# One routed tile's weight loads, a small tile's fetch and a routing table at other places in an attention and experts kernel

## The chip, the cores and the metric

The program runs on one core of a Trainium2 chip. The metric is the time of one execution in microseconds of the device, the median of several runs. One execution was also taken by the hardware profiler; all times inside the program are from that one, in microseconds from the start of its span.

TensorE is called PE in the views (PEld for its weight loads), VectorE DVE, ScalarE ACT, GpSimd POOL and SyncE SP. SP computes nothing here; it issues DMAs, in the order of the program.

## What is computed

Three stages, in float32: attention with rotated queries and keys (2 batches, 8 heads, 576 positions, 64 wide), a dense layer pair with softplus between, and a routed layer: every one of the 1,152 tokens with a positive score goes to one of 8 experts, and its expert's result is added to it.

```python
def _moe2_ref(x, w_skip, w_gate, w1, w2):
    do_compute = x @ w_skip > 0
    out = x.copy()
    xc = x[do_compute]
    logits = xc @ w_gate
    e_idx = np.argmax(logits, axis=1)
    probs = softmax(logits)
    gate_w = probs[np.arange(len(xc)), e_idx]
    for e in range(E):
        mask = e_idx == e
        h = np.maximum(xc[mask] @ w1[e], 0.0)      # w1[e]: 512 x 1024
        y[mask] = gate_w[mask, None] * (h @ w2[e]) # w2[e]: 1024 x 512
    out[do_compute] = xc + y
    return out
```

(`softmax` stands for the four lines that compute it.)

## The kernel before

Attention and the dense pair fill the first 380 us and are not touched. The rows that the dense pair gives are written to a table in DRAM, `x2d` (each with its gate and its number behind it), 128 rows at a time, and to `out`.

**Routed tiles.** Tokens are sorted by expert into tiles of 128 rows. A tile has one expert. What is left of an expert over full tiles and is at most 32 rows goes into small tiles, four parts of an expert's width by 32 rows. The program has seven full tiles in its straight path (tile 0 and tiles 1 to 6) and two small ones; further ones stand behind a branch. Which expert a tile has is known only when the routing is done: SP reads two values of `ei` for a tile, the expert and whether it differs from the tile before (`values`, L1184).

**Weights.** An expert's weights are eight chunks of 512 KB, in eight buffers `raw[0]` to `raw[7]`: 0 to 3 are of w1, 4 to 7 of w2. `load_chunk` (L947) issues one DMA on SP's queue. `load(T, chunks)` (L973) does so under the condition that tile T has another expert than T - 1; otherwise the DMA moves nothing, but it still is issued in its turn and waits for its buffer. Four further buffers, `sraw`, are for the small tiles.

A product in full precision is made of three with shorter operands. So a chunk is split: ScalarE copies its high half (`split_w`, L959), VectorE subtracts that from the chunk for the low half (`low_w`, L967). Chunk 0 of tiles 1 and later is used as it lies (`AS_IS`), in a slower product. A tile's rows are fetched from `x2d` by an indirect DMA of GpSimd (`fetch`, L979; `small_fetch` for a small tile), turned by PE (`rows`, `xgt` in the views), and copied by ScalarE: 128 columns whole (`xgw`, for chunk 0), the others split (`xgT`, VectorE making the low half).

**The passage** (`passage`, L798) lies between the dense pair and tile 1; in it the order on PE, VectorE, ScalarE and SP is the order of the code. It issues chunks 5, 6 and 7 (ahead of it) and `EARLY_RAW` of expert 0 for tile 0 and onward, routes the last two groups of 128 tokens (`route`, `ranks`), computes the places of all tokens (`cum`, `at`, `oht` on VectorE), multiplies with the tables `ohp` (one of 128 by 128 for each group, 1 at a token's rank) to get the rows of each tile (`idx`, `gi`), fetches tile 1's rows, writes `ei`, and meanwhile finishes tile 0's second product (`y`). The tables of the last two groups are made by GpSimd (`eng=nc.gpsimd`), all others by VectorE.

**The tiles' loop** (`tiles`, L1190) runs over T = 1 to 6. In one round PE makes T's first products (`mh`), then turns the next tile's rows, then makes the second products of T - 1 (`y`) around T's transposes (`ht`). SP's conditional loads for T + 1 and T + 2 and the splits stand at fixed places between. GpSimd's queue holds, in order, fetches and the outputs (`out_dram<-yo`). `SMALL` says which step of a small tile stands in which round: the first small tile is loaded in round 1 (`l0`), turned and multiplied in round 2 (`sxt`, `smh`), finished in round 3; the second in rounds 4 to 6.

Of the kernel before, what the change touches and what calls it, by code (L numbers as in the profile page):

```python
# [46 lines left out]
ORDER2 = (4, 5, 6, 7, 8, 0, 1, 2, 3)  # L47

AS_IS = (0,)
EARLY_RAW = (0, 1, 2)  # L50
HOLD = ((3, 15),)
EARLY = ((2, 11), (3, 10), (3, 11), (3, 12), (3, 13))
XGT = (3, 13)
# [586 lines left out]
class Moe2:  # L640
# [96 lines left out]
    def ranks(self, t0, n, sc, oh, pr, small, eng=None, between=((),) * 4):  # L737
        nc, c = self.nc, self.cst
        ts_ = slice(t0, t0 + n)
        rk, rd, rm = small("rk", 1), self.rd[:, ts_, :], small("rm", 1)  # L740

        def others(k):
            for do in between[k]:
                do()

        nc.vector.tensor_mul(sc[:, :, 0:8], oh, pr)
        others(0)
        with nc.allow_low_precision(reason="whole numbers"):
            nc.vector.tensor_reduce(rd, sc[:, :, 0:8], axis=AX.X, op=ALU.add)
        others(1)  # L750
        nc.vector.tensor_single_scalar(rd, rd, 0xFF80, op=ALU.bitwise_and)
        nc.vector.tensor_reduce(rk, sc[:, :, 0:8], axis=AX.X, op=ALU.add)
        others(2)

        nc.vector.tensor_sub(rm, rk, rd)
        for t in range(n):
            (eng or nc.vector).tensor_scalar(
                self.ohp[:, t0 + t, :], c["iota"], rm[:, t, :], self.tok[:, t0 + t, :], op0=ALU.is_equal, op1=ALU.mult
            )
        others(3)  # L760
# [39 lines left out]
    def passage(self, st, mh, xp, ps_x, ps_y, ps_h, psa):  # L800

        nc, c, ST, SS, sb = self.nc, self.cst, self.ST, self.SS, self.sp
# [7 lines left out]

        for k in EARLY_RAW:
            self.load_chunk(self.raw[k], 0, k)
# [23 lines left out]
        def y(k, x, z):  # L836
            for j in range(2):
                o = 128 * (2 * (k - 4) + j)
                n[0] += 1
                nc.tensor.matmul(  # L840
                    py, lhsT=ht[:, x, o : o + 128] if k < 7 else whole[:, 128 * j : 128 * j + 128],
                    rhs=(w[k][:, z] if k < 7 else self.raw[7])[:, 512 * j : 512 * j + 512],
                    start=n[0] == 1, stop=n[0] == 20,
                )
# [12 lines left out]
        def row(x):  # L857
# [4 lines left out]
            a, cnt.unsqueeze(1).to_broadcast([128, 2, 8]), c["up"].unsqueeze(2).to_broadcast([128, 2, 8]), op=ALU.add  # L862
        )
        ranks(eng=nc.gpsimd, between=(
            [partial(v.tensor_single_scalar, a, a, 0xFF80, op=ALU.bitwise_and)],
            [partial(v.tensor_copy, full, a[:, 0]), partial(v.tensor_sub, f[:, 1, 1:9], a[:, 1], a[:, 0])],
# [57 lines left out]
        v.tensor_scalar(self.e[:, ST:], ps, 0.0, c["far"], op0=ALU.is_equal, op1=ALU.mult)  # L924
        v.tensor_scalar(self.e[:, ST:], self.e[:, ST:], float(self.G), c["part"], op0=ALU.mult, op1=ALU.add)
        self.values(1)
        for k in (3, 4):
            self.load_chunk(self.raw[k], 0, k)
        self.load(1, 1, 2, 3, 0, 4)
        self.split_w(1, 1, 2, low=False)  # L930

        y(7, 0, 0)
        y(5, 0, 0)
# [8 lines left out]
        v.tensor_sub(w[6][:, 1], self.raw[6], w[6][:, 0].bitcast(F32))  # L942
        st = self.gather(1, xp, ps_x)
        y(6, 0, 1)
        self.split_w(1, 3, low=False)
        self.low_w(1, 1, 2, 3)
        return st, partial(self.finish, 0, xg, py, xp)  # L947

# [216 lines left out]
    def small(self, n, xp, ps_x, ps_y, ps_h, ps_a):  # L1165

        self.small_load(n, 0)
        self.small_fetch(n, xp)
        xt = self.small_copy(n, self.small_x(n, ps_x), xp)
        hs = self.small_hidden(n, xt, xp, ps_a)  # L1170
        self.small_load(n, 1)
        ht = self.small_copied(n, self.small_turn(n, hs, ps_x), xp)
        self.small_result(n, ht, xp, ps_a)()
# [17 lines left out]
    def tiles(self, Ts, xp, ps_x, ps_y, ps_h, ps_a, start=None, small={}):  # L1191
# [19 lines left out]
        def step(T, what):  # L1211

            for x in small.get(T, ()):
                if x[0] == what:
                    return int(x[1])

        for T in Ts:
            if (new := step(T, "l")) is not None:
                self.small_load(new, 0)
            pool, tag = ps_h[T % 2]  # L1220
            ph = [pool.tile([128, 512], F32, name=f"mh{T}{c}", tag=tag) for c in range(2)]
            mms = self.hidden_mm(T, st, ph)
# [50 lines left out]
                    self.split_w(T, 4)  # L1273
            if T + 2 <= last:
                self.fetch(T + 2, xp)
            if new is not None:
                self.small_fetch(new, xp)
            st, half = self.turn(T, st, xp, ps_x)
            if T > Ts[0] or T == last:
                mms, py = iter(()), None  # L1280
# [316 lines left out]
```

## Time and profile before

| | us |
|---|---|
| median of 3 runs | 506.09 |
| lowest and highest | 505.11, 506.34 |
| the profiled execution | 505.94 |
| its span in the trace | 503.8 |
| PE busy in it | 474.8 |
| VectorE, ScalarE, GpSimd busy | 371.4, 332.2, 127.8 |

A row of a timeline gives the start, the time until the last of its merged instructions ended, the engine, the line of the code, the operation, what is written from what, and how many instructions are merged; in brackets the idle time of the engine just before, and what ended it. Rows that follow each other may overlap, since an engine takes up an instruction before the one ahead has ended. An issue of a DMA (SPq) is over in a fraction of a microsecond; the transfer runs on 16 DMA engines and lands later. The granted clock (PEclk) is 1.00 at 2.4 GHz and 0.50 at 1.2 GHz.

### The profile page before, as it was taken

The page shows a single profiled execution, that of the slowest core. Times are in us where ns is not written, and L with a number is a line of the kernel's source. Part 1 is how long each engine was busy: PE and PEld are TensorE (multiplying, and loading weights), DVE is VectorE, ACT ScalarE, POOL GpSimd, SP SyncE. Part 2 cuts the span into 40 slices and gives each one's busy share as a digit, 9 for nine tenths or more (in the row PEclk, how much of TensorE's full clock was granted, in tenths as well). Part 3 has the DMA queues.
Part 4 walks back from the last instruction along what each step waited for, and adds up shares of the span by engine and source line. Part 5 has one row for each costly group of instructions (what it writes and reads, how often), then busy time and mean ns, then how long its engine had stood idle before and what let it go on. Part 6 is the DMA issues. An engine that isn't in the chain of part 4 may idle for free. (4 is left out here: it accounts for less than half of the span.)

```text
span 503.8 us, 8826 instructions
## 1 busy us (share of the span) xinstructions
PE 474.8 (94%) x3049; PEld 383.6 (76%) x3049; DVE 371.4 (74%) x697; ACT 332.2 (66%) x782; POOL 127.8 (25%) x167
## 2 busy tenths in 40 slices
PE   7999999999999999999999999999999698999991
PEld 3777768776676778999998998998987476777781
DVE  7676776688986986799989875538775756988660
ACT  2666776767767677977777677766773456867450
POOL 0965877756212300000000000001201221622011
PEclk9999999999999999999999999999999998999997
DMA  7578537547551320334433330502246442984411
GB/s 177 156 186 202 129 97 200 131 133 194 145 148 44 121 100 0 96 114 126 123 107 97 101 120 20 189 1 87 67 140 238 128 188 66 342 297 158 156 38 38
DMA packets 41509, 65.49 MB, mean 130 GB/s; under 512 B 9087, under 2 KB 23679, under 8 KB 41456
## 3 DMA queue, kind: packets, MB, share of 16 engines
q1 hardware_dynamic: 38480, 59.99, 39.2%
q0 software_dynamic: 1344, 4.20, 2.5%
q10 hardware_dynamic: 1632, 0.66, 0.6%
q8 instruction: 26, 0.43, 0.3%
q14 instruction: 27, 0.22, 0.1%
HBM read 67.32 MB, written 6.76 MB: 147 GB/s over the span
## 5 line engine op out<-in xcount | busy, mean ns | idle before, releaser
L590 PE MATMUL h<-xh,w 128*128 128x320 f32 (+2 forms) x464 | 104.2, 309 | 0.8 <-ACT rb L95 0.8
L628 PE MATMUL acc<-w,gh 128*128 128x512 f32 x288 | 80.7, 397 | 1.0 <-ACT gh L618 1.0
L590 PEld LDWEIGHTS h<-xh,w 128*128 128x128 f32 x464 | 78.0, 188 | 4.7 <-ACT rb L95 1.1
L590 PE MATMUL h<-xl,w 128*128 128x320 f32 (+2 forms) x232 | 69.2, 308 | 0.0
L269 DVE TENSOR_REDUCE m<-s 128x1 f32<-128x576 f32 x64 | 48.0, 754 | 19.9 <-PE s L260 16.6
L628 PEld LDWEIGHTS acc<-w,gh 128*128 128x128 f32 x288 | 51.8, 188 | 11.6 <-ACT gh L618 2.8
L971 DVE TENSOR_TENSOR ws<-raw,ws 128x1024 fp32r<-128x1024 f32 x42 | 49.5, 1220 | 9.0 <-ACT ws L964 8.9
L282 ACT ACTIVATE P<-s,m 128x576 f32<-128x576 f32 x64 | 47.6, 749 | 12.6 <-DVE m L269 12.3
L603 ACT ACTIVATE y<-h 128x320 f32<-128x320 f32 (+2 forms) x58 | 25.4, 438 | 41.1 <-PE h L590 39.8
L702 POOL TENSOR_SCALAR sc<-lg 128x2 f32<-128x2 f32 (+1 forms) x3 | 0.9, 292 | 201.3 <-DVE lg L685 201.3
L351 PE MATMUL t<-ct,P 128*128 128x128 f32 x288 | 45.6, 277 | 2.5 <-ACT pt L95 2.5
L964 ACT CAST ws<-raw 128x1024 fp32r<-128x1024 f32 x42 | 41.6, 1049 | 7.9 <-DMA raw<-in_moe_w_dram 7.9
L628 PE MATMUL acc<-w,gl 128*128 128x512 f32 x144 | 45.9, 392 | 0.0
L260 PE MATMUL s<-ks,qs 128*128 128x288 f32 x224 | 43.7, 317 | 2.1 <-ACT P L282 1.7
L590 PEld LDWEIGHTS h<-xl,w 128*128 128x128 f32 x232 | 43.2, 188 | 2.0
L619 DVE TENSOR_TENSOR gl<-r,gh 128x256 fp32r<-128x256 f32 (+2 forms) x42 | 25.8, 613 | 25.7 <-ACT gh L618 25.5
L351 PEld LDWEIGHTS t<-ct,P 128*128 128x128 f32 x288 | 33.6, 140 | 9.6 <-issue 3.4
L95 ACT COPY pt<-t 128x384 f32<-128x384 f32 x60 | 28.1, 480 | 18.1 <-PE t L351 17.9
L637 PE MATMUL y<-ws,hT 128*128 128x512 f32 x144 | 37.9, 407 | 0.0
L395 PE MATMUL pv<-pt,vr 128*64 128x256 f32 (+1 forms) x256 | 37.1, 412 | 0.0
L637 PE MATMUL mh<-ws,xgT 128*128 128x512 f32 x132 | 36.9, 421 | 0.0
L260 PEld LDWEIGHTS s<-ks,qs 128*128 128x128 f32 x224 | 31.6, 189 | 6.9 <-ACT P L282 3.6
(305 smaller groups left out, 946.8 us busy)
## 6 DMA issues: line engine op xcount, KB each, us to landing
raw<-in_moe_w_dram SPq DMA_DIRECT2D x56, 512.0 KB
raw<-in_moe_w_in_dram SPq DMA_DIRECT2D x16, 512.0 KB
raw<-in_moe_w_out_dram SPq DMA_DIRECT2D x16, 512.0 KB
sraw<-in_moe_w_dram SPq DMA_DIRECT2D x16, 512.0 KB
ks<-kT SPq DMA_DIRECT2D x28, 288.0 KB
qs<-qT SPq DMA_DIRECT2D x28, 128.0 KB
wr<-in_moe_w_dram SPq DMA_DIRECT2D x5, 512.0 KB
x2d<-x SPq DMA_DIRECT2D x9, 256.0 KB
```

The source lines that it names most:

```text
L95: self.nc.scalar.copy(out, in_)
L260: nc.tensor.matmul(ps[:, c, 0:288], lhsT=qs[:, a, uc], rhs=ks[:, a, x, 288 * c : 288 * c + 288], start=x == 0, stop=x == 1,)
L269: self.last = nc.vector.tensor_reduce(st["m"][:, a : a + 1], st["ps"][a][:, :, 0:288], axis=AX.XY, op=ALU.max, negate=True)
L282: nc.scalar.activation(P[:, 576 * a : 576 * a + 576].rearrange("p (c n) -> p c n", c=2), ps[:, :, 0:288], AF.Exp, bias=m[:, a : a + 1], ac ...
L351: self.tail = nc.tensor.transpose(ps[:, 128 * i : 128 * i + 128], src, ident)
L395: nc.tensor.matmul(ps[r, 0:n], lhsT=v, rhs=pt[:, k, 0:n], start=i < 0, stop=i == 3, skip_group_check=True,)
L590: nc.tensor.matmul(ps[c][:, 0:m], lhsT=w[:, 0, x, 128 * k : 128 * k + 128], rhs=src[:, k, c0 + m * c : c0 + m * c + m], start=z == 0, stop ...
L619: self.last = nc.vector.tensor_sub(gl, r, gh.bitcast(F32))
L628: nc.tensor.matmul(acc[t], lhsT=g[x][:, 128 * j : 128 * j + 128], rhs=w[:, 1, y, :], start=f == f0 and z == 0, stop=f == f1 and z == 2,)
L637: mm()
L964: self.nc.scalar.copy(self.w[T, c][:, 0], self.raw[c] if raw is None else raw)
L971: self.nc.vector.tensor_sub(w[:, 1], self.raw[c] if raw is None else raw, w[:, 0].bitcast(F32))
```

## The change

1. `EARLY_RAW` holds chunks 0 to 4 instead of 0 to 2, so chunks 3 and 4 of expert 0 are issued at the passage's beginning and no longer after `values(1)`.
2. Tile 1's conditional loads are issued in the order 0, 1, 2, 3, 4 instead of 1, 2, 3, 0, 4.
3. ScalarE copies tile 1's rows (`gather`) after the split of chunk 1 and ahead of that of chunk 2, instead of after both.
4. Of the last two groups' tables `ohp` the second is made by VectorE; the first stays with GpSimd.
5. `small_fetch` stands at the beginning of the round in which the small tile's loads are issued, instead of behind the outputs and fetches of that round.

```diff
-EARLY_RAW = (0, 1, 2)
+EARLY_RAW = (0, 1, 2, 3, 4)
...
-            (eng or nc.vector).tensor_scalar(
+            (nc.vector if t else eng or nc.vector).tensor_scalar(
                 self.ohp[:, t0 + t, :], c["iota"], rm[:, t, :], self.tok[:, t0 + t, :], op0=ALU.is_equal, op1=ALU.mult
             )
...
         self.values(1)
-        for k in (3, 4):
-            self.load_chunk(self.raw[k], 0, k)
-        self.load(1, 1, 2, 3, 0, 4)
-        self.split_w(1, 1, 2, low=False)
+        self.load(1, *EARLY_RAW)
+        self.split_w(1, 1, low=False)
...
         st = self.gather(1, xp, ps_x)
         y(6, 0, 1)
-        self.split_w(1, 3, low=False)
+        self.split_w(1, 2, 3, low=False)
         self.low_w(1, 1, 2, 3)
...
             if (new := step(T, "l")) is not None:
                 self.small_load(new, 0)
+                self.small_fetch(new, xp)
...
             if T + 2 <= last:
                 self.fetch(T + 2, xp)
-            if new is not None:
-                self.small_fetch(new, xp)
```

On SP's queue the passage stands like this before (`raw0` to `raw4` are the chunks' buffers, `x22` and `x23` rows of the dense pair, `gt2` their gates; an `ISA` ahead of a load sets its condition):

```order
L953 DMA raw2_4981<-in_moe2_w1_dram 128x1024
L1470 DMA x2d_63<-x22_4907 128x512
...
L778 DMA x2d_63<-gt2_5033 128x16 x2
...
L953 DMA raw3_4982<-in_moe2_w1_dram 128x1024
L957 DMA raw4_4983<-in_moe2_w2_dram 128x2x512
L953 ISA
L953 DMA raw1_4980<-in_moe2_w1_dram 128x1024
L953 ISA
L953 DMA raw2_4981<-in_moe2_w1_dram 128x1024
...
L953 DMA raw3_4982<-in_moe2_w1_dram 128x1024
L953 ISA
L953 DMA raw0_4979<-in_moe2_w1_dram 128x1024
```

and now:

```order
L951 DMA raw2_4981<-in_moe2_w1_dram 128x1024
L951 DMA raw3_4982<-in_moe2_w1_dram 128x1024
L955 DMA raw4_4983<-in_moe2_w2_dram 128x2x512
L1467 DMA x2d_63<-x22_4907 128x512
...
L778 DMA x2d_63<-gt2_5035 128x16 x2
...
L951 ISA
L951 DMA raw0_4979<-in_moe2_w1_dram 128x1024
L951 ISA
L951 DMA raw1_4980<-in_moe2_w1_dram 128x1024
L951 ISA
L951 DMA raw2_4981<-in_moe2_w1_dram 128x1024
```

The two unconditional loads moved ahead of the writes of `x2d`, and the conditional load of chunk 0 from behind that of chunk 3 to the first place.

On GpSimd's queue, from the tables on, before (`xg1` to `xg4` are the rows of tiles 1 to 4, `sxg0` those of the first small tile, `yo0` the result of tile 0):

```order
L757 TENSOR_SCALAR ohp_2402<-ct_65,rm2_5085,tok_2399 128x128 x2
L984 DMA xg1_5120<-x2d_63,gi_5117 128x528
L984 DMA xg2_5245<-x2d_63,gi_5117 128x528
L1076 DMA out_0_dram<-yo0_5327,si0_5325 1152x512
L984 DMA xg3_5338<-x2d_63,gi_5117 128x528
L1178 DMA sxg0_5342<-x2d_63,gi_5117 128x528
L984 DMA xg4_5433<-x2d_63,gi_5117 128x528
```

and now:

```order
L757 TENSOR_SCALAR ohp_2402<-ct_65,rm2_5087,tok_2399 128x128
L982 DMA xg1_5122<-x2d_63,gi_5119 128x528
L982 DMA xg2_5245<-x2d_63,gi_5119 128x528
L1176 DMA sxg0_5283<-x2d_63,gi_5119 128x528
L1074 DMA out_0_dram<-yo0_5331,si0_5329 1152x512
L982 DMA xg3_5342<-x2d_63,gi_5119 128x528
L982 DMA xg4_5433<-x2d_63,gi_5119 128x528
```

One table is gone from this engine, and the small tile's fetch moved from behind tile 3's rows to ahead of tile 0's output. In rounds 4 and 5 the second small tile's fetch moves in the same way ahead of tile 2's output, the first small tile's output and tile 6's rows.

On ScalarE, behind the splits of tile 0's chunks, before (`ws11`, `ws12`, `ws13` are the high halves of tile 1's chunks, `xgw1` and `xgT10` its rows):

```order
L964 CAST ws11_5202<-raw1_4980 128x1024
L964 CAST ws12_5204<-raw2_4981 128x1024
L1011 COPY xgw1_5231<-xgt1_5224 128x128
L1012 CAST xgT10_5229<-xgt1_5224 128x384
L964 CAST ws13_5237<-raw3_4982 128x1024
```

and now:

```order
L962 CAST ws11_5202<-raw1_4980 128x1024
L1009 COPY xgw1_5229<-xgt1_5222 128x128
L1010 CAST xgT10_5227<-xgt1_5222 128x384
L962 CAST ws12_5235<-raw2_4981 128x1024
L962 CAST ws13_5237<-raw3_4982 128x1024
```

The two copies of the rows moved ahead of one split. On PE the order is the same; on VectorE the one table is added behind `rm`, ahead of the steps that lead to `oht`.

## Rows read from the trace of the kernel before

**Rows 1.** Timeline of PE: the two idle stretches and two durations

```profile
401.44 3.60 PE L637 MATMUL mh<-raw,xgw 128*128 128x512 f32 x4 [3.43 <-DMA raw<-in_moe_w_dram]
...
409.52 1.88 PE L637 MATMUL mh<-raw,xgw 128*128 128x512 f32 x4
...
418.90 1.08 PE L1093 MATMUL sxt<-ct,sxg 128*128 128x128 f32 x4 [2.44 <-DMA sxg<-x2d,gi]
...
487.54 5.87 PE L637 MATMUL y<-ws,hT 128*128 128x512 f32 x24
```

**Rows 2.** Busy time by stretch: length, PE, PEld, DVE, ACT, POOL, granted clock, DMA share, GB/s

```profile
401.35:404.76 3.41, 3.32 (x5) 1.51 (x5) 1.45 (x3) 1.96 (x3) 0.00 (x0) 0.50 0.03 8
418.41:421.83 3.42, 2.93 (x11) 2.76 (x12) 0.22 (x1) 1.16 (x4) 0.00 (x0) 0.50 0.25 74
422.00:493.00 71.00, 71.00 (x481) 53.56 (x480) 54.57 (x69) 45.45 (x63) 17.90 (x9) 1.00 0.49 180
```

**Rows 3.** Timeline of SP's queue: chunks of tile 1 and 2, then the small tile's

```profile
394.72 0.34 SPq L953 DMA_DIRECT2D raw<-in_moe_w_dram  x1
...
395.86 0.48 SPq L953 DMA_DIRECT2D raw<-in_moe_w_dram  x2
...
400.90 0.43 SPq L953 DMA_DIRECT2D raw<-in_moe_w_dram  x2
...
403.39 0.96 SPq L953 DMA_DIRECT2D raw<-in_moe_w_dram  x3
405.15 1.95 SPq L953 DMA_DIRECT2D sraw<-in_moe_w_dram  x4
```

**Rows 4.** Timeline of POOL: two tables, fetches, tile 0's output, tile 1's output

```profile
389.54 1.65 POOL L757 TENSOR_SCALAR ohp<-ct,rm,tok 128x128 f16<-128x128 f32 x2 [2.53 <-DVE sb L744]
392.74 1.12 POOL L984 DMA_INDIRECT xg<-x2d,gi  x1 [1.55 <-ACT ws L809]
...
411.70 1.97 POOL L1076 DMA_INDIRECT out_dram<-yo,si  x1 [16.52 <-DVE yo L1075]
413.98 1.03 POOL L984 DMA_INDIRECT xg<-x2d,gi  x1 [0.30 <-issue]
415.31 1.00 POOL L1178 DMA_INDIRECT sxg<-x2d,gi  x1 [0.31 <-issue]
...
432.25 6.29 POOL L1076 DMA_INDIRECT out_dram<-yo,si  x1 [14.63 <-DVE yo L1075]
```

**Rows 5.** Fetches of `xg`, issue to landing: tile 2's (394.17), then tile 3's (413.98)

```profile
DMA to landing us min/median/max: 6.2/6.2/6.2
...
DMA to landing us min/median/max: 3.2/3.2/3.2
```

**Rows 6.** Timeline of ACT: splits of tile 1's chunks 1 and 2, its rows

```profile
395.96 2.00 ACT L964 CAST ws<-raw 128x1024 fp32r<-128x1024 f32 x2 [3.95 <-DMA raw<-in_moe_w_dram]
397.87 0.25 ACT L1011 COPY xgw<-xgt 128x128 f32<-128x128 f32 x1
```

**Rows 7.** Timeline of DVE: low halves of tile 1, tile 0's result

```profile
399.01 2.35 DVE L971 TENSOR_TENSOR ws<-raw,ws 128x1024 fp32r<-128x1024 f32 x2
...
410.67 0.74 DVE L1075 SCALAR_TENSOR_TENSOR yo<-y,xg 128x512 f32<-128x512 f32 x1
```

**Rows 8.** Timeline of DVE: an earlier pair of tables; steps towards `oht` in the passage

```profile
368.89 0.59 DVE L757 TENSOR_SCALAR ohp<-ct,rm,tok 128x128 f16<-128x128 f32 x2
...
389.91 0.23 DVE L876 TENSOR_TENSOR sb<-sb,cum 128x72 f32<-128x72 f32 x1
...
390.92 0.38 DVE L883 TENSOR_TENSOR oht<-least,at 128x207 f16<-128x207 f32 x1
```

**Rows 9.** Busy time by stretch, columns as in rows 2: the DMA's load

```profile
375.00:386.00 11.00, 10.57 (x58) 8.33 (x57) 4.97 (x12) 3.98 (x11) 0.00 (x0) 1.00 0.95 373
386.00:390.00 4.00, 3.72 (x37) 2.88 (x36) 3.09 (x23) 2.31 (x7) 1.25 (x5) 1.00 0.05 7
...
406.00:412.20 6.20, 6.20 (x27) 4.38 (x27) 3.08 (x5) 3.37 (x6) 0.50 (x1) 1.00 0.88 333
```

## The prediction

> **What bounds the kernel now.** I read the timeline of TensorE (PE) around the start of the routed tiles first, since the two moved groups of instructions sit there. It has two long idle stretches [rows 1]. The first ends at 401.44: PE was through with tile 0 at 401.44 - 3.43 = 398.0 and stood until the first product of tile 1, which reads weight chunk 0 as it lies. The second ends at 418.90: PE was through with tile 2's first products at 418.90 - 2.44 = 416.46 and stood for the rows of the small tile (`sxg`). Next I read the granted clock in short windows [rows 2]. Behind each idle stretch the clock is at its lower level (0.50, 1.2 GHz), 3.41 us each time, with 3.32 and 2.93 us of PE work in them. Work that takes 3.32 us there takes 1.66 at full clock, so 1.66 and 1.46 us are lost on top of the idle time. From 422 to 493 PE is busy 71.00 of 71.00 us at full clock: whatever is gained before 422 goes through to the end unless a new wait appears.
>
> Why the two waits are so long is told by the queues. SP issues chunks 3 and 4 of expert 0 only at 394.72 and right behind, then the conditional loads of chunks 1 and 2, and the next two (3, then 0) not before 400.90 [rows 3]. The conditional load of chunk 3 writes the buffer into which the load of 394.72 is still running, so SP stands from 395.86 + 0.48 = 396.3 to 400.9, and chunk 0, which PE needs first, stands behind it. Chunk 0 itself had been in place all along: the conditional loads move nothing here. The four after 400.90 cannot have carried data, since the DMA share is 0.03 in 401.35 to 404.76 [rows 2]; tile 1 has tile 0's expert. On GpSimd (POOL) the small tile's fetch of 415.31 stands behind tile 0's output (411.70) and the fetch of tile 3's rows (413.98) [rows 4]; PE starts on its rows 3.6 us after it.
>
> **The change, part by part.**
>
> First stall. Chunks 3 and 4 now go out behind chunk 2, near 376, and conditional chunk 0 is the first to be issued after the two values are read, near 394.72 + 0.25 + a quarter for its registers, 395.2; the five follow in steps of some 0.4 us (two in 0.48 and in 0.43 [rows 3]), all buffers filled long ago. So PE waits for the copied rows (`xgw`) instead. In [rows 6] ScalarE copies them at 397.87, right behind the splits of chunks 1 and 2 (395.96 + 2.00), of which the second now stands behind. PE makes the rows just ahead of its last products, so the copy cannot come much sooner: it ends near 398.1 to 398.3 with the shift below, and PE starts some 0.1 us after its last product. Is tile 1 then short of split weights? The low halves on VectorE take 2.35 for two [rows 7], and would be ready at 400.5, 401.7 and 402.9; PE starts at 398.35, needs 1.88 us for the chunk read as it lies (409.52 in [rows 1], at full clock) and 0.245 us for each product of split weights (24 in 5.87 at 487.54 [rows 1]), and so wants them at 401.2, 402.6 and 404.4. Slack 0.7 us or more, no wait. This stall gives 3.43 + 1.66 - 0.1.
>
> The table on VectorE. POOL takes 1.65 for two tables [rows 4], ending at 391.19; VectorE's `oht`, on which the same products wait, ends at 391.30. VectorE took 0.59 for two such tables [rows 8], so one adds 0.25 (0.2 to 0.3) to the later of the two paths, and POOL, off the path, ends 0.8 sooner. I book a loss of 0.25 us. By the rows alone a gain is excluded: the later path gets longer.
> How VectorE fares beside POOL's other table is shown by its 72-element step of 389.91, 0.23 us while POOL was at its tables [rows 8]: not held up. The Trainium skill, "SBUF — State Buffer", section "Who interferes with whom", says that a tensor_scalar on VectorE can hold the port pair that it shares with GpSimd, and that the second of the two then blocks entirely. By that rule VectorE's table would end 0.83 us later if POOL's starts first, and the total would be 498.7 instead of 497.9; the row shows no blocking for another kind of operation, so I keep 0.25 and give the other case a chance (B).
>
> The early loads. They add 1 MB to a stretch that is already full: DMA share 0.95, 373 GB/s from 375 to 386 [rows 9]; 1 MB at 373 GB/s is 2.8 us. Behind them wait the writes of x2d's last 256 rows and, through them, the fetch of tile 1's rows at 392.74 [rows 4]. That traffic is over by 386 (share 0.05 from 386 to 390 [rows 9]), so now by 389: 3.7 us remain, and I book nothing. PE, ScalarE and VectorE read nothing of chunks 3 and 4 before 399. SP's two more issues (0.34 and about 0.43 us) fall in a time in which SP waits for those rows. With chunks 3 and 4 no longer in flight at 394 to 400, the rows of tiles 1 and 2 rather land sooner: tile 2's fetch took 6.2 us to land, tile 3's 3.2 [rows 5].
>
> Second stall. The small tile's fetch moves ahead of tile 0's output, near 395.7, and lands by about 400; PE wants it at 411.7. It pushes nothing back: the output is ready only after VectorE's step of 410.67 [rows 7]. What is late next is tile 3's rows. They were issued at 413.98 and landed 3.2 us later [rows 5], at 417.2; with the small rows there, PE would have wanted them at 416.46 + some 0.4 for the small tile's transposes (1.08 at most, at the lower clock [rows 1]) = 416.8. Everything from tile 1 on moves together, so 0.4 us of wait remains. One thing moves less: the four loads for the small tile (405.15 [rows 3]), whose traffic runs to 412.2 (0.88 share [rows 9]). They follow by 0.8 us the three conditional loads of 403.39 + 0.96, the last of which waits for tile 1's low halves, now at 402.9: 403.8, some 1.4 us sooner, while tile 3's fetch comes 4.7 sooner, near 409.2. Its first 1.6 us then fall into the end of that traffic. Between no effect (3.2 us to land) and 6.2 - 3.2 = 3.0 more, I take 0.2 more, since only the end overlaps: 0.6 us of wait. Short gaps left the clock up: 1.00 from 386 to 390 with PE busy 3.72 of 4.00 us [rows 9]. The stall gives 2.44 + 1.46 - 0.6 = 3.3.
>
> The other small tile's fetch, at tile 4, moves up one place too; PE does not wait there, and I book nothing.
>
> **Sum.** 3.43 + 1.66 - 0.1 - 0.25 + 3.3 = 8.04 us. The profiled execution took 505.94 us (span 503.8), against a median of 506.09, so the two are the same for this purpose: 505.94 - 8.04 = 497.9 us. Best case, nothing left of either wait and a free table: 3.43 + 1.66 + 2.44 + 1.46 = 8.99, 496.95 us; the runs of before spread half a microsecond to one side.
>
> **Rivals.**
> A, tile 3's rows come late and the second stall stays. For it: a POOL output issued under full DMA traffic took 6.29 us, not 1.97 [rows 4], and now the first output runs under the small tile's loads; or the fetch takes 6.2 us to land. Against it: this output took its 1.97 us partly under the same traffic, and the fetch behind it 1.03. With 3.0 us more, PE idles 3.4 us, begins tile 3's transposes at 415.5 instead of about 419.8 (418.90 and most of the 1.08 there), 4.3 sooner, and the lower clock costs up to 0.6 more than what was left of it before: a gain of 3.7 to 4.3, 501.6 to 502.2 us. With 4.3 us more (6.29 for 1.97): 503 to 503.6 us.
> B, VectorE's table waits for POOL's: 0.83 us more on the path, 498.7 us. Against: the 0.23 us rows above.
> C, the gain is given back further on, since weights are split by VectorE, which is busy 54.57 of 71 us [rows 2]. It would need a new wait of 6.5 us or more to come within 0.3% of before (504.6 to 506). Against: the loads and splits there are released by earlier splits and products, which move along by the same 8 us.
> D, slower: SP's two early loads stand ahead of the x2d rows. If their buffers were still in use, SP would wait there with the rows behind it, and tile 1's fetch would start late; PE has nothing else from 398 on. From 3.7 us of delay on each microsecond costs one, and after 3.7 + 8 = 11.7 us the kernel is slower: with 14 us, 508.2 us. Against: in the new order these two loads carry no wait for a compute engine beyond those of the six chunks ahead of them.
>
> **How the numbers follow.** Forecast 0.72, 496.4 to 499.5 (the bounds of the table, of the last waits, and the spread of the runs). A 0.17, B 0.04, C 0.04, D 0.03. The range is to hold 8 in 10: the forecast's range with B holds 0.76, and the milder half of A brings it over, so 496.4 to 502.2. About 0.3% (1.5 us) is what a measurement of this kernel can tell from no change; the forecast, A and B are faster by more (0.93), C is the same (0.04), D is slower (0.03).
>
> **What would show it.** Right: PE's first product of tile 1 on chunk 0 at 398 to 398.6 with no DMA wait ahead, tile 1's products done near 405 instead of 409.7, clock 1.00 from 398 to 412, the small fetch near 395.7 on POOL, tile 3's transposes near 412.6, and PE's last product near 485.4 instead of 493.4. Wrong: `idx` products later than 391.8 (B); a wait of 2 us or more ahead of tile 3's transposes with a clock of 0.50 behind it (A); new idle time on PE after 422 (C); tile 1's fetch later than 393.5 (D).

## The result and the profile after

The changed kernel takes 501.12 us (median of six runs, 499.46 to 502.12), the kernel before in the same session 505.48 us (six runs, 504.48 to 506.34). The ratio is 0.9908, with a 95% interval of 0.9885 to 0.9932: faster by 4.4 us. The forecast was 497.9 us with a range of 496.4 to 502.2; the sign and the range held, but little more than half of the forecast gain of 8.04 us came.

The profiled execution of the changed kernel took 502.12 us with a span of 499.9, against 505.94 and 503.8: 3.8 us less. First the timeline of PE from tile 0's second product to tile 3's transposes:

```profile
389.78 1.20 PE L840 MATMUL y<-ws,hT 128*128 128x512 f32 x4 [0.28 <-ACT hT L828]
392.03 0.39 PE L890 MATMUL idx<-oht,ohp 128*128 128x15 f16 x9 [1.04 <-DVE oht L883]
...
393.01 3.19 PE L840 MATMUL y<-raw,hTw 128*128 128x512 f32 x4
395.22 4.22 PE L840 MATMUL y<-ws,hT 128*128 128x512 f32 x12
...
399.63 0.71 PE L840 MATMUL y<-ws,hT 128*128 128x512 f32 x2
400.23 1.98 PE L637 MATMUL mh<-raw,xgw 128*128 128x512 f32 x4
...
408.33 1.96 PE L637 MATMUL mh<-raw,xgw 128*128 128x512 f32 x4 [1.49 <-DMA raw<-in_moe_w_dram]
...
415.19 0.60 PE L1091 MATMUL sxt<-ct,sxg 128*128 128x128 f32 x4
415.62 0.60 PE L996 MATMUL xgt<-ct,xg 128*128 128x128 f32 x4
...
482.36 5.87 PE L637 MATMUL y<-ws,hT 128*128 128x512 f32 x24
```

The row of 400.23 answers to the first row of [rows 1]: tile 1 starts with no bracket behind it, so the stall of 3.43 us is gone. The row of 415.19 answers to the third: the 2.44 us for the small tile's rows are gone too, and tile 3's rows (415.62) are not waited for either. Three things are worse than before. PE idles 1.04 us ahead of `idx`, where it was 0.52; tile 2's first product on chunk 0 waits 1.49 us (before, at 409.52 in [rows 1], nothing); and two groups of `y` take 3.19 and 4.22 us, which took 1.98 and 3.35 in the passage of before (its rows stand further down).

The windows of the changed kernel (columns as in [rows 2]) tell why the last two are longer:

```profile
390.24:393.65 3.41, 2.10 (x51) 1.36 (x50) 2.72 (x17) 1.93 (x3) 0.63 (x2) 1.00 0.02 5
393.65:397.06 3.41, 3.41 (x7) 1.67 (x6) 3.37 (x10) 0.90 (x1) 2.80 (x3) 0.50 0.43 97
397.06:406.84 9.78, 9.78 (x42) 6.81 (x41) 6.32 (x8) 5.62 (x10) 0.28 (x1) 1.00 0.20 54
406.84:408.33 1.49, 0.00 (x1) 0.03 (x1) 1.49 (x3) 1.49 (x3) 0.00 (x0) 1.00 0.90 313
408.33:488.00 79.67, 79.67 (x522) 60.06 (x522) 59.93 (x75) 51.01 (x73) 21.55 (x12) 1.00 0.54 191
```

Behind a stretch in which PE was busy 2.10 of 3.41 us the clock is at 0.50 (1.2 GHz) for 3.41 us, fully used; that costs about 1.7. It stays at 1.00 behind both places where it fell before ([rows 2]), and from 408.33 to 488 PE is not idle at all: nothing is given back later.

The untouched part before the passage, and what lies behind PE's last product, differ from one execution to the next. Here are the rows of the passage in the kernel before:

```profile
389.63 1.20 PE L840 MATMUL y<-ws,hT 128*128 128x512 f32 x4 [0.28 <-ACT hT L828]
391.35 0.39 PE L890 MATMUL idx<-oht,ohp 128*128 128x15 f16 x9 [0.52 <-DVE oht L883]
...
392.34 1.98 PE L840 MATMUL y<-raw,hTw 128*128 128x512 f32 x4
393.76 3.35 PE L840 MATMUL y<-ws,hT 128*128 128x512 f32 x12
...
397.30 0.71 PE L840 MATMUL y<-ws,hT 128*128 128x512 f32 x2
```

So I measure each traced execution from the start of these `y` products to the end of PE's last: before 487.54 + 5.87 - 389.63 = 103.78 us, after 482.36 + 5.87 - 389.78 = 98.45. That is 5.33 us less, and the single rows account for it:

| | us |
|---|---|
| first stall and the half-clock stretch behind it gone | -3.43 - 1.66 |
| second stall and the half-clock stretch behind it gone | -2.44 - 1.46 |
| idle ahead of `idx`, 1.04 instead of 0.52 | +0.52 |
| half clock from 393.65 | +1.66 (read from `y` below) |
| wait for tile 2's chunk 0 | +1.49 |
| sum | -5.32 |

For the half clock: from the start of the first long group of `y` to that of the products behind `xgt` PE takes 399.63 - 393.01 = 6.62 us here and 397.30 - 392.34 = 4.96 in the kernel before, at full clock there, so 1.66. The whole execution gained only 3.8 because PE's end was followed by 499.9 - 488.23 = 11.7 us against 503.8 - 493.41 = 10.4, and 0.15 were lost ahead of the passage. About 1.0 of these 1.3 us lies ahead of GpSimd's last output, issued at 493.60 after and at 497.81 before, 5.4 and 4.4 us behind PE's end. In the eleven kernels traced below that last stretch is 11.0 to 11.6 us; why it was 10.4 in the one traced execution of before is not settled.

### The profile page after: what moved, and what is told of

The parts are those of the page before. It is cut to its first block, busy times and chain, and to the rows that moved or that the text cites. A ratio compares the mean times of both kernels' runs of the same rounds, so it can differ in the third digit from the quotient of the medians.

```text
span 499.9 us, 8824 instructions
## 1 busy us (share of the span) xinstructions
PE 473.1 (95%) x3048; PEld 382.2 (76%) x3049; DVE 371.1 (74%) x698; ACT 332.2 (66%) x782; POOL 127.2 (25%) x166
```

## The experiments

Each kernel was timed in alternation with the kernel before. Experiments 1 to 4 shared one session (before: 504.64 us, 20 runs), 5, 6, 8 and 9 a second (506.20, 12 runs), 7, 10 and 11 a third (506.08, 17 runs), and the changed kernel has the session of the result; so ratios are compared, not times. "PE" is the length defined above, in one traced execution.

| | edit | us | ratio, 95% interval | PE |
|---|---|---|---|---|
| after | the whole change | 501.12 | 0.9908 (0.9885 to 0.9932) | 98.45 |
| 1 | after, both tables on GpSimd | 498.86 | 0.9870 (0.9837 to 0.9903) | 96.28 |
| 2 | after, small loads behind chunk 0 | 501.57 | 0.9930 (0.9902 to 0.9959) | 99.12 |
| 3 | 1 and 2 | 501.10 | 0.9904 (0.9870 to 0.9938) | 100.53 |
| 4 | before, small fetch early | 501.59 | 0.9940 (0.9914 to 0.9965) | 97.33 |
| 5 | before, order of loads | 502.89 | 0.9929 (0.9899 to 0.9959) | 99.88 |
| 6 | before, early loads | 500.03 | 0.9879 (0.9844 to 0.9913) | 97.63 |
| 7 | before, one table on VectorE | 505.46 | 0.9988 (0.9964 to 1.0013) | 102.98 |
| 8 | after, idle time filled | 499.59 | 0.9871 (0.9841 to 0.9900) | 96.80 |
| 9 | 3, rows fetched earlier | 497.53 | 0.9827 (0.9792 to 0.9862) | 94.57 |
| 10 | 4 and 6 | 498.66 | 0.9861 (0.9835 to 0.9887) | 96.28 |
| 11 | 9, idle time filled | 498.09 | 0.9854 (0.9826 to 0.9882) | 95.36 |

My theory: the two stalls went as forecast; what is missing is a new queue place (chunk 0 of tile 2 behind the small tile's loads) and the table, which lengthens an idle time and with it brings the lower clock. The rivals: the table has no part in the clock; or weights and rows crowd each other on the DMA engines, whichever goes first.

**1. The table back to GpSimd.**

```diff
-            (nc.vector if t else eng or nc.vector).tensor_scalar(
+            (eng or nc.vector).tensor_scalar(
```

> The changed kernel with one part undone: both tables of the last two groups are made by GpSimd again. Theory (the table on VectorE lengthens the path to the idx products, PE stands 1.04 us ahead of them instead of 0.52, and the lower clock that follows at 393.65 is a result of that gap): the gap ahead of idx is back at 0.5 us, the clock stays 1.00 from 386 to 406, tile 0's products end near 398.2 instead of 400.3, and the time falls by 0.5 us or, where the clock had fallen, by 2.2 us. Rival (the lower clock falls in that place whatever the gap): the gap shrinks by 0.5 us and the clock is 0.50 somewhere in 386 to 400 all the same; the time falls by 0.5 us. The wait of 1.5 us ahead of tile 2's first product stays in both.

The timeline of PE in this kernel:

```profile
390.89 0.38 PE L890 MATMUL idx<-oht,ohp 128*128 128x15 f16 x9 [0.52 <-DVE oht L883]
...
391.88 1.98 PE L840 MATMUL y<-raw,hTw 128*128 128x512 f32 x4
...
405.54 1.96 PE L637 MATMUL mh<-raw,xgw 128*128 128x512 f32 x4 [1.49 <-DMA raw<-in_moe_w_dram]
```

The idle time is 0.52 again, the long `y` group 1.98, the clock is 1.00 to PE's end, and the wait for chunk 0 is unchanged. All five runs lie between 498.15 and 499.09. In the two traces PE's length is 98.45 - 96.28 = 2.17 us shorter without the fourth part, 0.52 of it by the idle time and 1.66 by the clock. By the ratios the part costs about 1.9 us, but their intervals overlap a little. Nor does this one trace show that the clock fell because of the table; experiments 2, 3 and 7 bear on that.

**2. Chunk 0 ahead of the small tile's loads.**

```diff
             if (new := step(T, "l")) is not None:
-                self.small_load(new, 0)
                 self.small_fetch(new, xp)
...
                 self.load(T + 1, 0)
+            if new is not None:
+                self.small_load(new, 0)
             self.load(T, 6, 7)
```

> The changed kernel, but the small tile's value and its four loads stand on SP's queue behind the conditional load of the next tile's chunk 0, at the end of the round, and no longer at its beginning. Theory (PE's new wait of 1.49 us at 408.33 is for the conditional load of tile 2's chunk 0, which moves nothing but is issued only at 408.13 because the small tile's four issues, 1.94 us, stand ahead of it): that load is issued right behind tile 2's chunks 1 to 3 and a load of tile 1, near 405.5, PE's wait is gone, 1.5 us faster. Rival (the load waits for its buffer, which PE's products on chunk 0 hold, or for the chunks ahead of it, which VectorE releases): PE's wait shrinks by less than 0.5 us.

The timeline of PE, and one window (columns as in [rows 2]):

```profile
404.53 1.88 PE L637 MATMUL mh<-raw,xgw 128*128 128x512 f32 x4
...
414.14 0.84 PE L996 MATMUL xgt<-ct,xg 128*128 128x128 f32 x4 [2.23 <-DMA xg<-x2d,gi]
```

```profile
405.00:411.00 6.00, 6.00 (x29) 4.46 (x28) 4.75 (x7) 3.94 (x7) 3.69 (x3) 1.00 0.98 365
414.41:417.83 3.42, 3.42 (x13) 2.74 (x12) 1.69 (x2) 1.59 (x3) 0.00 (x0) 0.50 0.00 0
```

Tile 2 has no wait left, which confirms the place in the queue as the cause of the 1.49 us. But the kernel is no faster: tile 3's rows, fetched at 408.98 while the DMA engines are busy to 0.98, take 5.0 us to land, PE waits 2.23 us for them, and the clock falls behind it. That is a wait of rival A's kind. The wait for chunk 0 had hidden some 0.9 us of it: in the changed kernel these rows were fetched at 411.13 and landed 3.9 us later, at 415.0, and without the 1.49 us PE would have wanted them at 415.62 - 1.49 = 414.1 (an estimate). The rest fits this edit itself, which also puts the small tile's loads later, 404.05 - 398.07 = 5.98 us behind tile 1's first product instead of 405.46 - 400.23 = 5.23, so that more of their traffic is left when the rows are fetched.

**3. Both.** The edits of 1 and 2 together.

> The changed kernel with both of the edits of the two runs ahead: both tables with GpSimd, and the small tile's loads behind tile 2's chunk 0. If both theories hold: PE without a stall of over 0.6 us from 386 on, the clock 1.00 until PE's last product, 2 us faster than the changed kernel where its clock stays up, 3.7 us where it falls: 497.5 to 499 us. If only the chunk's holds: 1.5 to 2 us faster than the changed kernel, with a stretch at clock 0.50 left.

```profile
390.40 0.39 PE L890 MATMUL idx<-oht,ohp 128*128 128x15 f16 x9 [0.52 <-DVE oht L883]
...
391.39 3.44 PE L840 MATMUL y<-raw,hTw 128*128 128x512 f32 x4
...
414.89 0.63 PE L996 MATMUL xgt<-ct,xg 128*128 128x128 f32 x4 [2.42 <-DMA xg<-x2d,gi]
```

The wait for tile 3's rows is there again (2.42), and the clock is at 0.50 behind it. So neither of the two expected times came: 501.10 us. And in this execution the clock fell in the passage (3.44 instead of 1.98) with only 0.52 us idle ahead of `idx`. So the longer idle time is not needed for the fall; experiment 2, whose clock stayed up behind 1.03 us idle at that place, shows that it is not enough either.

**4. The small tile's fetch alone**, in the kernel before.

```diff
                 self.small_load(new, 0)
+                self.small_fetch(new, xp)
...
-            if new is not None:
-                self.small_fetch(new, xp)
```

> The kernel before with one part of the change alone: the small tile's fetch at the beginning of the round. Theory (the second stall is this fetch alone, and the next thing late, tile 3's rows, costs under 0.6 us): PE's stall of 3.4 us at 401 stays with its stretch of lower clock, the one of 2.44 us at 418.9 falls to 0 to 0.6 us, its stretch of lower clock goes, and the time falls by 3.3 to 3.9 us, to 501.6 to 502.2. Rival (tile 3's rows or the output take its place): the stall shrinks by less than 1.5 us and the lower clock stays, 503.5 us or more.

```profile
399.94 1.95 PE L637 MATMUL mh<-raw,xgw 128*128 128x512 f32 x4 [1.90 <-DMA raw<-in_moe_w_dram]
...
414.32 0.63 PE L998 MATMUL xgt<-ct,xg 128*128 128x128 f32 x4 [0.36 <-DMA xg<-x2d,gi]
```

The second stall is down to 0.36 us, for tile 3's rows, as the prediction had it (0.6). The first was 1.90 in this execution instead of 3.43, without a fall of the clock behind it: SP got through its four conditional issues in 3.94 us (from 395.88) instead of 5.47 (from 395.86), so the late chunk 3 seems to have landed sooner. The kernel gained 504.64 - 501.59 = 3.05 us, a little less than the 3.3 to 3.9 expected.

**5. The order of the loads alone**, in the kernel before.

```diff
-        self.load(1, 1, 2, 3, 0, 4)
+        self.load(1, 0, 1, 2, 3, 4)
```

> The kernel before with one edit: tile 1's conditional loads in the order 0, 1, 2, 3, 4; chunks 3 and 4 of expert 0 are still issued late. Theory (PE's first stall was chunk 0's place behind a conditional load that waits for chunk 3 in flight): PE starts tile 1 on chunk 0 near 398.4 without a wait for it, but the conditional load of chunk 3 still stands until about 400.9, its copy ends near 402.5 and its low half near 404, so PE waits up to 0.8 us there; the second wait (2.4 us) stays: about 4 to 4.5 us faster than before, 500.5 to 501.5 us. Rival (the early loads are what removes the stall): PE waits 2 us or more in tile 1, 503 to 505 us.

PE's timeline, then SP's:

```profile
398.71 1.98 PE L637 MATMUL mh<-raw,xgw 128*128 128x512 f32 x4 [0.52 <-ACT xgw L1011]
...
408.16 3.53 PE L637 MATMUL mh<-raw,xgw 128*128 128x512 f32 x4 [2.83 <-ACT ws L964]
```

```profile
396.02 4.88 SPq L953 DMA_DIRECT2D raw<-in_moe_w_dram  x4
...
407.96 0.08 SPq L953 DMA_DIRECT2D raw<-in_moe_w_dram  x1
```

Tile 1 no longer waits for chunk 0, but SP still stands at the conditional load of chunk 3 (four issues take 4.88 us), and everything behind it on SP is late. The bill is paid at tile 2's chunk 0: issued at 407.96, 0.20 us before PE starts on it, as in the changed kernel (408.13 and 408.33). The view names ScalarE, which ended last, but the copied rows that this product reads were done at 405.76; the issue fits. My expected 0.8 us at chunk 3 did not show, and neither did the second wait of 2.4 us, since PE came to the small tile's rows late, at 416.59. The clock fell behind the 2.83 us (the products on chunk 0 take 3.53 us instead of 1.98), and the time lay above what the theory gave.

**6. The early loads alone**, in the kernel before.

```diff
-EARLY_RAW = (0, 1, 2)
+EARLY_RAW = (0, 1, 2, 3, 4)
...
-        for k in (3, 4):
-            self.load_chunk(self.raw[k], 0, k)
```

> The kernel before with one edit: chunks 3 and 4 of expert 0 issued early; the conditional loads stay in the order 1, 2, 3, 0, 4. Theory: with chunk 3 long in place nothing holds SP, the four conditional issues go out in 1.6 us from 395.2 on, chunk 0's near 396.8, before PE wants it at 398: the first stall goes as fully as with both edits; the second wait (2.4 us) stays: 500.5 us (499.5 to 501.5). Rival (the order is what removes it): PE waits 1 us or more for chunk 0, 502 to 504 us. A second rival: the added 1 MB delays the fetch of tile 1's rows beyond 393.5, then PE waits for these rows.

```profile
398.05 1.98 PE L637 MATMUL mh<-raw,xgw 128*128 128x512 f32 x4
...
406.13 1.96 PE L637 MATMUL mh<-raw,xgw 128*128 128x512 f32 x4 [1.46 <-DMA raw<-in_moe_w_dram]
...
414.27 0.63 PE L1091 MATMUL sxt<-ct,sxg 128*128 128x128 f32 x4 [1.11 <-DMA sxg<-x2d,gi]
```

This one edit removes the first stall whole, with chunk 0 still fourth in the order. The second wait is shorter (1.11) because the wait for chunk 0, ahead of it, takes part of it over. Tile 1's rows were fetched at 392.88: the added 1 MB delayed nothing. On PE this one edit is 98.45 - 97.63 = 0.82 us shorter than the whole change; by the ratios the two can't be told apart.

**7. The table alone**, in the kernel before.

```diff
-            (eng or nc.vector).tensor_scalar(
+            (nc.vector if t else eng or nc.vector).tensor_scalar(
```

> The kernel before with one edit: the second of the last two tables on VectorE. Theory (the table lengthens the path to idx by 0.5 us and exposes the passage to the lower clock): the idle time ahead of idx is 1.04 us instead of 0.52, the time 0.5 us over before if the clock stays 1.00 behind it and up to 2.2 over if it falls, so a ratio of 1.001 to 1.004. Rival (the 0.5 us is hidden here by PE's long wait for chunk 0, which ends by SP's queue and not by idx): within 0.1% of before, and the wait for chunk 0 shorter by 0.5 us.

```profile
391.86 0.39 PE L890 MATMUL idx<-oht,ohp 128*128 128x15 f16 x9 [1.04 <-DVE oht L883]
```

The idle time ahead of `idx` was 1.04 us, and the clock did not fall behind it (the first long group of `y` took 1.98 us). The wait for chunk 0 was 3.68, and the ratio covers both no cost and the 0.5 us of the theory. It tells only that here the table does not bring a further 1.7 us in most runs; the rival's shorter wait was not seen either. Inconclusive.

**8. The idle time filled**, in the changed kernel.

```diff
+        extra = ps_h[1][0].tile([128, 512], F32, name="extra_mm", tag=ps_h[1][1])
+        for z in range(4):
+            nc.tensor.matmul(extra, lhsT=ht[:, 0, 0:128], rhs=w[4][:, 0, 0:512], start=z == 0, stop=z == 3)
         pi = psa.tile([128, 512], F32, name="idx", tag="ra")
```

> The changed kernel with one edit: four products of 128x512 that nothing reads are put on PE ahead of those for idx, into the idle time there. Theory (the idle 1.04 us ahead of idx, after a passage with many short gaps, is what let the clock fall in 393.65 to 397.06): PE shows no idle time over 0.4 us there, the granted clock stays 1.00 until tile 2, and the time is 499.4 us (498.9 to 500.2) against 501.1 of the changed kernel. Rival (the clock falls there for another reason, as it fell once with the shorter gap of 0.52 us): 0.50 shows again behind idx, time 501 to 502 us.

PE's timeline and a window over the passage (columns as in [rows 2]):

```profile
389.72 1.09 PE L890 MATMUL extra_mm<-ws,hT 128*128 128x512 f32 x4
390.92 0.39 PE L894 MATMUL idx<-oht,ohp 128*128 128x15 f16 x9
...
391.91 1.98 PE L840 MATMUL y<-raw,hTw 128*128 128x512 f32 x4
```

```profile
388.00:404.00 16.00, 15.35 (x105) 10.44 (x103) 13.33 (x40) 9.45 (x15) 4.24 (x4) 1.00 0.24 57
```

With useless work in the gap the clock stays up in this execution, and PE's length is 98.45 - 96.80 = 1.65 us shorter. All six runs lie between 499.24 and 500.29. Of the changed kernel's six, two lie there as well (499.46 and 499.50, mean clock 0.991 and 0.993) and four at 501.06 to 502.12 with a mean clock of 0.989. So the fall seems not to be in every run of the changed kernel: that is what its mean clocks say, though only one of the six has a trace here. That the filling is what keeps the clock up is suggested by this and not shown: experiments 2 and 7 had the same gap unfilled and no fall in their traces.

**9. All waits at once.** Experiment 3, and the fetch of the rows of tile T + 2 at the beginning of round T.

```diff
                 self.small_fetch(new, xp)
+            if T + 2 <= last:
+                self.fetch(T + 2, xp)
             pool, tag = ps_h[T % 2]
...
-            if T + 2 <= last:
-                self.fetch(T + 2, xp)
             st, half = self.turn(T, st, xp, ps_x)
```

> The changed kernel with three edits: both last tables on GpSimd again, the small tile's four loads behind the load of the next tile's chunk 0, and the fetch of the rows two tiles ahead moved to the beginning of the round, so that it is issued ahead of tile 0's output and ahead of the small tile's loads. Theory (the new waits of the change are places in queues, each to be had without the other): no wait of 0.5 us or more on PE between tile 0's last product and tile 3's first; idle time ahead of the products for idx near 0.5 us; about 2.3 us less than the changed kernel by the table and 1.5 more by chunk 0, so 497 us (496 to 498.2), or 1.7 more for each stretch at half clock if one shows. Rival (rows and weights crowd each other whichever goes first): one of the two waits stays or moves to tile 2's rows, 498.5 to 501 us.

GpSimd's queue, then PE's timeline and a window from the passage on:

```profile
396.03 1.00 POOL L982 DMA_INDIRECT xg<-x2d,gi  x1 [0.30 <-issue]
```

```profile
403.43 1.88 PE L637 MATMUL mh<-raw,xgw 128*128 128x512 f32 x4
...
410.66 0.60 PE L996 MATMUL xgt<-ct,xg 128*128 128x128 f32 x4
```

```profile
388.00:483.00 95.00, 93.92 (x623) 69.87 (x621) 74.67 (x115) 61.83 (x89) 25.50 (x17) 1.00 0.52 174
```

PE waits for no DMA any more in this stretch: tile 3's rows are fetched at 396.03, ahead of the small tile's loads (402.94). PE is busy 93.92 of 95.00 us. This kernel is 9.2 us shorter on PE than before and faster than both kernels: its ratio of 0.9827 (0.9792 to 0.9862) lies clear of the changed kernel's (0.9885 to 0.9932). Its six runs fall into 495.46 to 496.71 and 498.36 to 498.91.

**10. The early loads and the early fetch, nothing else.** The edits of 4 and 6 in the kernel before.

> The kernel before with two edits: chunks 3 and 4 of expert 0 issued early, and the small tile's fetch at the beginning of the round; the order 1, 2, 3, 0, 4 of the conditional loads, the place of the row copies and both tables on GpSimd are as before. Theory (the order of the loads and the place of the copies bring nothing once chunk 3 is in place): as the changed kernel with both tables on GpSimd, a ratio of 0.987 (0.984 to 0.990), with the wait of 1.5 us for tile 2's chunk 0 in it. Rival (they bring the 0.3 to 0.5 us by which the copied rows are ready sooner): a wait for the copied rows of 0.3 us or more ahead of tile 1, a ratio of 0.988 or more.

PE's length is 96.28, the same as in experiment 1, which has the other two parts (order of the loads, place of the copies) besides; the ratios, 0.9861 and 0.9870, agree. No wait for the copied rows appeared ahead of tile 1. So two of the five parts carry the gain, two bring nothing beside them, and one (the table) costs 0.5 us on PE, and more in an execution whose clock falls.

**11. Experiment 9 with its idle time filled**, by two products.

```diff
+        extra = ps_h[1][0].tile([128, 512], F32, name="extra_mm", tag=ps_h[1][1])
+        for z in range(2):
+            nc.tensor.matmul(extra, lhsT=ht[:, 0, 0:128], rhs=w[4][:, 0, 0:512], start=z == 0, stop=z == 1)
```

> The kernel with tables on GpSimd, the small tile's loads behind chunk 0 and the rows fetched a round's length earlier, and two products of 128x512 that nothing reads in the idle time of 0.53 us ahead of idx. Theory (single runs of the kernel without them lost 1.7 us or more to a fallen clock, as its mean clock of 0.988 beside 0.993 shows; the filled gap keeps it up): the highest of the runs comes down, median 496.5 us (495.5 to 497.2), ratio 0.981. Rival (what falls is elsewhere, or the products push idx back): the same spread and 497.5 us, ratio 0.983.

The runs moved together (497.93 to 498.56), so the highest came down, but the lowest went up and the median is no better. The traced execution has a new wait of 0.64 us:

```profile
429.09 0.63 PE L1053 MATMUL ht<-ct,hs 128*128 128x128 f32 x4 [0.64 <-DVE xgT L1015]
```

Whether the fill has to do with it, and whether the two groups of runs in experiment 9 differ by a fallen clock, stays open.

## Why the prediction was right, and where it failed

**The first stall: right.** Tile 1 starts behind tile 0's last product, and 5.09 us are gone. Experiment 6 shows that the reason given, SP held by the load of chunk 3 in flight, is enough: with it gone, the new order of the loads, which the prediction counted on equally, is not needed. Experiment 5 shows that the order alone also takes the wait for chunk 0 away from tile 1 (0.52 us for the copied rows is left), but it leaves SP held, and tile 2 pays.

**The early loads at no cost: right.** Tile 1's rows were fetched 1.4 us behind the start of `idx` (393.42 and 392.03) as before (392.74 and 391.35).

**The second stall: gone, with more than was booked.** 0.6 us of wait for tile 3's rows was forecast and none is there, but for a bad reason: PE came 1.49 us later. Without that some 0.9 us would have been left (experiment 2). Experiment 4 has the forecast residue (0.36); experiments 2 and 3, which also move the small tile's loads, have more (2.23 and 2.42).

**"Everything from tile 1 on moves together": the step that failed first.** SP's queue in the changed kernel:

```profile
402.41 2.24 SPq L951 DMA_DIRECT2D raw<-in_moe_w_dram  x3
405.46 1.94 SPq L951 DMA_DIRECT2D sraw<-in_moe_w_dram  x4
...
408.13 0.08 SPq L951 DMA_DIRECT2D raw<-in_moe_w_dram  x1
```

The row of 408.13 is the conditional load of tile 2's chunk 0. It stands behind the small tile's four loads, and these behind three loads that wait for tile 1's low halves on VectorE. The prediction had even worked out that these four move by only some 1.4 us while the rest moves by more, and used it for one consequence, the crowding of tile 3's rows. (In the trace they come no sooner at all, 405.46 against 405.15 in [rows 3], since the passage itself lost time.) It did not go on down SP's own queue to the next entry that PE needs. In the kernel before that entry came in time because PE was late itself; it wanted the chunk at 409.52 ([rows 1]):

```profile
407.83 0.08 SPq L953 DMA_DIRECT2D raw<-in_moe_w_dram  x1
```

The cost is 1.49 us; the load moves nothing and is ready 0.20 us after its issue, so it is the place that costs; with the load ahead of the small tile's four, the wait is gone (experiments 2 and 9).

**The table: 0.51 booked as 0.25.** VectorE in the kernel before, then in the changed one:

```profile
389.20 0.16 DVE L755 TENSOR_TENSOR rm<-rk,rd 128x2 f32<-128x2 f32 x1
389.27 0.23 DVE L744 TENSOR_TENSOR sb<-rd,cntf 128x72 f32<-128x72 int32 x1
```

```profile
389.36 0.16 DVE L755 TENSOR_TENSOR rm<-rk,rd 128x2 f32<-128x2 f32 x1
389.63 0.34 DVE L757 TENSOR_SCALAR ohp<-ct,rm,tok 128x128 f16<-128x128 f32 x1
389.89 0.22 DVE L744 TENSOR_TENSOR sb<-rd,cntf 128x72 f32<-128x72 int32 x1
...
391.59 0.38 DVE L883 TENSOR_TENSOR oht<-least,at 128x207 f16<-128x207 f32 x1
```

The table itself costs the 0.26 us until `sb` starts, as forecast. But it reads `rm`, made just ahead, and so starts 0.27 us after `rm`'s start, where before `sb`, which does not read it, started after 0.07 us. From `rm` to `oht` it is 2.23 us now against 1.72 (389.20, and 390.92 in [rows 8]). A step put into a chain costs its own time and the wait for what it reads.

Rival B did not happen, although `idx` came later than the 391.8 that was to show it. GpSimd's table ran beside VectorE's:

```profile
389.70 0.94 POOL L757 TENSOR_SCALAR ohp<-ct,rm,tok 128x128 f16<-128x128 f32 x1 [2.53 <-DVE rm L755]
```

A half of the pair in [rows 4] is 0.83, so neither engine lost more than about 0.1. The Trainium skill ("SBUF — State Buffer", section "Who interferes with whom") says that where a tensor_scalar on VectorE takes the port pair that it shares with GpSimd, the engine that issues second blocks fully until the first is done. By that and these rows GpSimd would have lost up to 389.63 + 0.34 - 389.70 = 0.27 us, an estimate; the trace shows no wait of that size.

**The clock: not foreseen.** The prediction took [rows 9], 386 to 390 at 1.00, as evidence that short gaps leave the clock up, and looked for falls only behind long stalls. In the changed kernel's trace the clock fell in the passage, and 1.66 us went for which the sum had no term. What brings this fall stays open. With 1.03 or 1.04 us idle ahead of `idx` it came in one trace of three (the changed kernel; not in experiments 2 and 7); with 0.52 to 0.54 us in one of eight (experiment 3; not in the kernel before nor in experiments 1, 4, 5, 6, 9 and 10); with the gap filled in neither of two (8 and 11). So the length of the gap does not decide alone. The mean clocks of experiment 8's runs (0.991 to 0.994, against 0.989 in four of the changed kernel's six) suggest that filling it helps, but one trace does not show it.

Together: 1.49 + 1.66 + 0.27 (the table) less 0.6 (the residue) and 0.1 (the wait for the copied rows, not seen) = 2.7 us, which is 8.04 - 5.33. The rest of the miss in the profiled execution, 1.5 us, lies ahead of the passage and behind PE's end.

**The range: held, and partly by luck.** The mechanism as forecast gave 496.4 to 499.5 us, and 501.12 is outside that. It lies in what was added for the milder half of rival A, a late fetch of tile 3's rows; but in the changed kernel PE does not wait for these rows. The other costs named here happened to be of that size.

## What to carry to other kernels

When a stall is removed on one engine, walk down every queue that serves it, entry by entry, and compare each entry's new time with the new time of its use: a queue that is paced by something else does not move along, and the first entry that was just in time is the next stall. Take one part of a composite change at a time where that is cheap; here two parts gave all of the gain and one took back 0.5 us, or 2.2 in an execution whose clock fell. An instruction added to a chain between two engines is priced by the start of what follows it, not by its duration.

## What the runs showed of the hardware

The clock's falls differ between executions of one kernel. Between 380 us and PE's end the traced execution of the kernel before has two falls, behind 3.43 and 2.44 us idle; experiment 4 had a wait of 1.90 us and no fall at all, experiment 7 one of 2.52 us without a fall behind it, and experiment 3 fell after an idle time of 0.52. A fall cost 1.5 to 1.7 us in this kernel, and the runs of before spread by several us in the first session, 502.15 us with a mean clock of 0.994 to 507.27 with 0.986.

An indirect fetch of 128 rows took 3.2 us to land (tile 3's in [rows 5]) and 6.2 while chunks 3 and 4 were in flight (tile 2's); for tile 3's rows it was 3.9 in the changed kernel, 5.0 in experiment 2, where more of the small tile's loads still ran, and 4.2 when issued ahead of them (experiment 9). What counts is the room ahead of its use: in experiment 9 it had 14 us.
